# List-ordered attention on one core: how the half blocks of the transposed weights are copied, and the durations of the ordering loop

## The chip, the core and the metric

The kernel runs on one NeuronCore of a Trainium2 chip. The metric is the device time of one execution in microseconds (us), the median of a few runs. The engines are named as the profile names them: PE is the matrix engine, PEld its weight loads, DVE the vector engine, ACT the scalar engine, POOL the general engine, SP the queue that issues nearly all DMAs.

## What is computed

Three layers one after the other: causal attention with a window of 128 and a linear bias, a soft mixture of experts, and a feed-forward layer with a squared relu. All data are fp32.

```python
scores = scale * np.matmul(q, k.transpose(0, 1, 3, 2))            # (4, 8, 576, 64)
mask = (rel >= 0) & (rel < window)                                # window = 128
scores = np.where(mask, scores + bias[None], -1000000000.0)
attn = np.exp(scores - np.max(scores, axis=-1, keepdims=True))
attn = attn / (np.sum(attn, axis=-1, keepdims=True) + 1e-09)
x = np.matmul(attn, v)                                            # then (2304, 512)
x = moe(x, phi, w1, w2)                                           # 8 experts of 4 slots
out = np.maximum(x @ w_in, 0.0) ** 2 @ w_out                      # d_ff = 2048
```

## The kernel before, in words

**The attention** works on 16 units `u` (4 batches by 4 pairs of heads). A unit has 9 chunks `c` of 64 queries for both heads, so a chunk fills 128 rows. 144 chunks are taken two at a time, in 72 steps `t`; a step can hold the last chunk of one unit and the first of the next. One step goes through these functions:

- `emit_S` (L174, PE): scores of the step's two chunks, up to 192 keys each, in a bank "S" (3 of them).
- `emit_max` (L181, DVE): adds the bias table, writes the negated scores into one of six `p` buffers, and takes the row minimum in the same operation (a second small instruction reads the accumulator out).
- `emit_exp` (L192, ACT): the exponential with its row sum.
- `emit_sums` (L198, POOL) and `emit_recip` (L203, DVE): sum and reciprocal, for two steps at once except at both ends.
- `emit_fold` (L208, POOL): of the 192 keys of a chunk the oldest 64 and the newest 64 are never allowed for the same query at the same place, so the oldest are subtracted from the newest. One block then holds the newest as positive and the oldest as negative numbers, and 128 columns are left to be transposed in place of 192.
- `emit_norm` (L222, POOL): multiplies by the reciprocal.
- `emit_T` (L230, PE): transposes each chunk's 128 columns into one bank "T" (3 of them), as `A[:, i, :]`; keys are now rows.
- `emit_evac` (L251): `(t, 0)` on ACT (L254) is a Relu over all 128 rows of both chunks into the slots of `ptb`: the whole block and the newest half. `(t, 1)` on DVE then brings the oldest half, which is negative, into its slot of another block: `max(-x, 0)` on 64 rows (L258). In an even chunk these are rows 0 to 63 and in an odd one rows 64 to 127. A unit's first chunk has no older keys and its only half is copied (L260).
- `emit_PV` (L262, PE): once all of a unit's blocks are there, 24 matmuls of weights by values, each over whole slots. The half of a slot that no copy fills was set to zero at the start (L406 to L408).

Chunks 2 to 8 of a unit have an oldest half, 112 in all; 48 steps hold two of them, 16 hold one. Behind `emit_PV` come copies of its result, transposes and the logits of the experts (L281 to L379).

**The order** of all this is not the program's text. Each call is an entry `op(f, arg, eng, ns, after, due, banks, lag, at)` (L412): engine, duration in ns, what it needs, a due time, the PSUM bank that it takes, and the lag from its end until another engine may use the result. `arrange()` (L485) is a list scheduler that runs when the program is built: it repeatedly takes the entry that could start first (then the earliest due), sets its engine's clock forward by `ns` and makes the result ready `lag` later. The sequence it returns is the program's order; every engine then executes its share strictly in that order (L558). DMA issues hang on calls (L538 to L555): the last `emit_S` of a unit issues the queries and keys of a later unit and two or three half weights of 512 KB, `emit_xTb` the values of a later unit.

```python
op(emit_evac, (t, 1), "DVE", 208 * len(half), each(emit_T, t) + each(emit_evac, (t, 0)) + free(half), t0 + 4300)
...
ready[x] = max(ready[x], seen[k])
```

**After the attention** come a short softmax over experts (L588 to L665), the matmuls with w1 (L739, "H") and w2 (L878, "O"), whose 1 MB weights come through a ring of 19 tiles and are loaded again as tiles get free, and the last layer (L916 to L1120), where w_in and w_out are unpacked on the way. When the last `emit_S`, the last `emit_T` and the whole attention are done, their buffers are freed and five more weights are loaded (L97).

Of the kernel before, what the change touches and what calls it, by code (L numbers as in the profile page):

```python
# [28 lines left out]
def attn_moe_relu2_kernel(ctx: ExitStack, tc: tile.TileContext, z, k, v, phi, w1, w2, w_in, w_out, bias, cst, out):  # L29
# [200 lines left out]
    def emit_T(t):  # L230
        full, rest, P = [], [], pbuf[t % NP]
        for u, c, n, e in info[2 * t:2 * t + 2]:
            if c == 0:
                rest.append((e, 0, jblk(u, 0), False))
            elif c % 2:
                full.append((jblk(u, c // 2) + 1, e + n - 128, (64, jblk(u, c // 2 - 1) + 3, True) if c > 1 else None))
            else:
                full.append((jblk(u, c // 2 - 1) + 2, e, (0, jblk(u, c // 2), True)))
        full.sort(key=lambda x: x[0])
        A = bank("T", "tp")[:, 0:256].rearrange("p (a b) -> p a b", a=2)  # L240
        for i, o in enumerate([x[1] for x in full] + [x[0] for x in rest]):
            pe.transpose(A[:, i, :], P[:, o:o + 128], ident)  # L242
        sl = [x[0] for x in full]
        st = sl[1] - sl[0] if len(sl) == 2 else 1
        half = [(i, *x[2]) for i, x in enumerate(full) if x[2]] + [(len(full) + i, *x[1:]) for i, x in enumerate(rest)]
        tp_t[t] = (ptb[:, sl[0]:sl[-1] + 1:st], A[:, 0:len(sl)]), [(ptb[r:r + 64, slot], A[r:r + 64, i], neg) for i, r, slot, neg in half]

    def jblk(u, j):
        return 4 * ((4 * u + j) % NBL) if j < 4 else 4 * NBL + u % 2
# [177 lines left out]
    for t in range(NS):  # L427
        ch, t0 = info[2 * t:2 * t + 2], STEP * t
        two = [(t, 0), (t, 1)]
        steps = (t,) if t in alone else (t - 1, t) if t % 2 else (t, t + 1)  # L430
        op(emit_S, t, "PE", sum(4 * n / 2.4 + 12 for u, c, n, e in ch), (), t0 - 1500, (("S", each(emit_max, *two)),), 170, max(x for y, x in landed.items() if y <= t))
        for i, (u, c, n, e) in enumerate(ch):
            op(emit_max, (t, i), "DVE", n / 0.96 + 72, each(emit_S, t) + each(emit_T, *range(t - NP, t - NP + 1)[:t >= NP]), t0 + 100 * i, (), 140)
            op(emit_exp, (t, i), "ACT", n / 1.4 + 303, each(emit_max, (t, i)), t0 + 400 + 100 * i)
        if t == steps[0]:
            op(emit_sums, (t, len(steps)), "POOL", 200, each(emit_exp, *[(x, i) for x in steps for i in range(2)]), STEP * steps[-1] + 1500)
            op(emit_recip, (t, len(steps)), "DVE", 110, each(emit_sums, (t, len(steps))), STEP * steps[-1] + 1600)
        whole = sum(x[2] == 192 for x in ch)
        if whole:
            op(emit_fold, t, "POOL", 182 + 138 * whole, each(emit_exp, *two), t0 + 1500)  # L440
        for i, (u, c, n, e) in enumerate(ch):
            eng = "DVE" if t >= NS - 2 and i == 1 else "POOL"
            op(emit_norm, (t, i), eng, 345 if n > 64 else 290, each(emit_recip, (steps[0], len(steps))) + each(emit_fold, t)[:whole], t0 + 1900 + 100 * i, (), 70)
        full = [(u, (c - 1) // 2) for u, c, n, e in ch if c]
        half = [(u, c // 2 if c % 2 == 0 else c // 2 - 1) for u, c, n, e in ch if c != 1]
        free = lambda l: each(emit_PV, *[owner[x] for x in l if owner[x] is not None])
        op(emit_T, t, "PE", 222, each(emit_norm, *two), t0 + 3500, (("T", each(emit_evac, *two[:1 + bool(half)])),), 170)
        op(emit_evac, (t, 0), "ACT", 80 + 100 * len(full), each(emit_T, t) + free(full), t0 + 4000)
        if half:
            op(emit_evac, (t, 1), "DVE", 208 * len(half), each(emit_T, t) + each(emit_evac, (t, 0)) + free(half), t0 + 4300)  # L450
    for u in range(NU):
        b, kk = divmod(u, NPAIR)
        t0, odd, late = STEP * fin[u], b % 2, u == NU - 1
        parts = [(t, i) for t in range(NCH * u // 2, fin[u] + 1) for i in range(2) if (emit_evac, (t, i)) in ops]
        old = (each(emit_X, u - 4) + each(emit_logr, (u - 4) // NPAIR)) if 4 <= u < NU - 4 + 2 else []
        op(emit_PV, u, "PE", 1840, each(emit_evac, *parts), t0 + 5500, (("xa", each(emit_xT, u)), ("T" if late else "B", each(emit_xTb, u))), 190, 9500)
        op(emit_xT, u, "ACT", 490, each(emit_PV, u) + old, t0 + 7400)
        op(emit_xTb, u, "DVE" if late else "ACT", 125, each(emit_PV, u) + old, t0 + 7450)
        if late:
            break  # L460
        x_all = each(emit_xT, u) + each(emit_xTb, u)
        if u < NU - 2:
            tag = "T" if kk == NPAIR - 1 else "B"
            op(emit_X, u, "PE", 436, x_all, t0 + 9000, ((tag, each(emit_xn, u)),), 170)
            op(emit_xn, u, "DVE", 608, each(emit_X, u) + each(emit_d3, b - 1)[:b], t0 + 9500)
            if odd:
                op(emit_Y, u, "PE", 109, each(emit_X, u), t0 + 9010, (("T", each(emit_xr, u)),), 170)
                op(emit_xr, u, "ACT", 175, each(emit_Y, u) + each(emit_d3, b - 1)[:b], t0 + 9500)
        if kk == NPAIR - 1 or u == NU - 2:
            us = range(NPAIR * b, u + 1)  # L470
            x_all = each(emit_xT, *us) + each(emit_xTb, *us)
            last_b = u == NU - 2
            op(emit_logits, b, "PE", 260 * len(us) + 100, x_all, t0 + 9500, () if last_b else (("B", each(emit_d0, b)),), 190)
            op(emit_logr, b, "PE", 110 * len(us), each(emit_logits, b), t0 + 9600, (), 190)
            if last_b:
                continue
            op(emit_d0, b, "ACT", 400, each(emit_logr, b), t0 + 10500)
            op(emit_d1, b, "DVE", 600, each(emit_d0, b), t0 + 11000)
            op(emit_de, b, "ACT", 760, each(emit_d1, b), t0 + 11500)
            op(emit_d2, b, "PE", 120 + 110 * odd, each(emit_de, b), t0 + 13000, (("T", each(emit_dn, b)),), 170)  # L480
            op(emit_dn, b, "DVE", 320, each(emit_d2, b), t0 + 13500)
            op(emit_d3, b, "PE", 1260 + 500 * odd, each(emit_dn, b) + each(emit_xn, *us) + each(emit_xr, *us) * odd, t0 + 14000, (("T", each(emit_d4, b)),), 190)
            op(emit_d4, b, "DVE", 650 + 200 * (b > 0), each(emit_d3, b), t0 + 15000)

    def arrange():  # L485
        wait = {k: len(o["after"]) for k, o in ops.items()}
        for k, o in ops.items():
            for x in o["after"]:
                users.setdefault(x, []).append(k)
        ready, seen, order = {k: o["at"] for k, o in ops.items()}, {}, []  # L490
        clock = dict.fromkeys(("PE", "DVE", "ACT", "POOL"), 0)
        held = {tag: [] for tag in NBUF}
        can = {e: [k for k in ops if ops[k]["eng"] == e and not wait[k]] for e in clock}

        def room(k):
            when = 0
            for tag, readers in ops[k]["banks"]:
                if len(held[tag]) >= NBUF[tag]:
                    for x in held[tag][len(held[tag]) - NBUF[tag]]:
                        if x not in seen:  # L500
                            return None
                        when = max(when, seen[x])
            return when

        while len(order) < len(ops):
            best = None
            for e in clock:
                for k in can[e]:
                    r = room(k)
                    if r is not None:  # L510
                        x = (max(clock[e], ready[k], r), ops[k]["due"], len(order), k)
                        if best is None or x[:2] < best[:2]:
                            best = x
            start, _, _, k = best
            o = ops[k]
            can[o["eng"]].remove(k)
            clock[o["eng"]] = start + o["ns"]
            seen[k] = start + o["ns"] + o["lag"]
            for tag, readers in o["banks"]:
                held[tag].append(readers)  # L520
            for x in users.get(k, ()):
                wait[x] -= 1
                ready[x] = max(ready[x], seen[k])
                if not wait[x]:
                    can[ops[x]["eng"]].append(x)
            order.append(k)
        return order
# [644 lines left out]
```

## Time and profile before

| | us |
|---|---|
| median of 3 runs | 401.55 (401.39 to 402.41) |
| the profiled execution's own time | 401.11 |
| its span, first to last instruction | 399.3 |
| first scores to the first matmul of H | 3.7 to 137.4 |
| H and O | 137.4 to 168.0 |
| last layer | from 172 to the end |

The profile tells for each engine when it was busy. "Idle before" is the time that an engine stood before an instruction, with what ended it. The chain is found from the last instruction back: at each step to what released it, or to the instruction before it on its engine. Where a timeline shows consecutive instructions of one engine, the distance from one start to the next is what the first one costs its engine, since an instruction's own duration overlaps with the next.

### The profile page before, as it was taken

To read this page: it belongs to the slowest core of one execution; us is meant where nothing else is said; L and a number is where in the kernel's file an instruction comes from. 1 tells how busy PE (TensorE), PEld (TensorE's weight loads), DVE (VectorE), ACT (ScalarE), POOL (GpSimd) and SP (SyncE) were. 2 spreads that over 40 slices of the span, in tenths; PEclk is the share of its full clock that TensorE was granted. 3 is DMA by queue.
4 is the path that set the end of the run, shared out by engine and by line. 5 is a ranking of instruction groups with operands and counts; after the bars stand their busy time and mean duration, and the time that the engine had idled before them with its cause. 6 is when DMAs were issued, how large, how long until landed. Compare 5 with 4: busy or idle time off the path is not lost.

```text
span 399.3 us, 7923 instructions
## 1 busy us (share of the span) xinstructions
PE 387.0 (97%) x2602; PEld 300.8 (75%) x2602; DVE 283.6 (71%) x862; ACT 244.2 (61%) x730; POOL 118.0 (30%) x291
## 2 busy tenths in 40 slices
PE   8899999999998999999999999999999999999996
PEld 7687778787875534687787888788877888888884
DVE  5687787778784685477877889786867874567445
ACT  4978879778883411178867765767666634443440
POOL 4858758657674041203111111111010000000000
PEclk9999999999998999999999999999999999999999
DMA  7989969889999999999502200000000040003004
GB/s 227 384 290 340 342 244 377 303 279 379 318 365 319 389 419 423 421 417 420 193 0 77 102 34 0 2 0 2 0 0 2 0 158 2 0 27 133 0 2 158
DMA packets 23225, 75.36 MB, mean 189 GB/s; under 512 B 2832, under 2 KB 4624, under 8 KB 21520
## 3 DMA queue, kind: packets, MB, share of 16 engines
q1 hardware_dynamic: 22608, 74.30, 49.8%
q10 hardware_dynamic: 576, 0.56, 0.4%
q8 instruction: 21, 0.34, 0.3%
q14 instruction: 20, 0.16, 0.1%
HBM read 70.13 MB, written 4.72 MB: 187 GB/s over the span
## 4 chain that ended last, share of the span: by engine, by line
PE 81%; DVE 7%; ACT 5%; issue 2%; POOL 2%; DMA 2%; DVEq 0%; SPq 0%; ACTq 0%; POOLq 0%
PE acc L975 49%; PE s L178 6%; PE xa L270 4%; PE h L931 4%; PE H L739 4%; PE O L878 4%; PE tp L242 3%; ACT p L196 3%; DVE ptb L258 2%; DVE p L187 2%; DMA kt<-in_k_dram 2%; POOL p L228 1%; PE MX L827 1%; DVE psum L993 1%; ACT ptb L254 1%
## 5 line engine op out<-in xcount | busy, mean ns | idle before, releaser
L975 PE MATMUL acc<-whl,arena_gh 128*128 128x512 f32 x864 | 216.5, 394 | 0.0
L975 PEld LDWEIGHTS acc<-whl,arena_gh 128*128 128x128 f32 x864 | 160.1, 188 | 35.3 <-issue 2.9
L960 DVE TENSOR_TENSOR arena_gh<-hT,arena_gh 128x384 fp32r<-128x384 f32 (+1 forms) x97 | 53.7, 553 | 29.7 <-ACT arena_gh L956 24.2
L196 ACT ACTIVATE p<-p,st 128x192 f32<-128x192 f32 (+1 forms) x144 | 61.5, 429 | 17.0 <-DVE st L187 15.4
L943 ACT ACTIVATE acc<-h 128x384 f32<-128x384 f32 x47 | 23.1, 493 | 64.9 <-PE h L931 64.9
L787 POOL TENSOR_SCALAR yw<-f 128x512 f32<-128x512 f32 x32 | 27.3, 857 | 99.0 <-DVE arena_cin L804 53.5
L178 PE MATMUL s<-kt,zq 128*128 128x192 f32 (+2 forms) x270 | 51.0, 323 | 2.3 <-DVE st L187 1.8
L228 POOL TENSOR_SCALAR p<-p,st 128x128 f32<-128x128 f32 (+1 forms) x142 | 49.8, 370 | 11.6 <-DVE st L206 10.5
L187 DVE CUSTOM_DVE_ANT_0 p<-s,tbl 128x192 f32<-128x192 f32 (+1 forms) x144 | 41.1, 325 | 7.3 <-PE s L178 4.4
L178 PEld LDWEIGHTS s<-kt,zq 128*128 128x128 f32 x270 | 41.6, 195 | 4.2 <-DVE st L187 3.0
L258 DVE TENSOR_SCALAR ptb<-tp 64x128 f32<-64x128 f32 x112 | 32.0, 286 | 8.8 <-ACT ptb L254 6.6
L242 PE MATMUL tp<-cs,p 128*128 128x128 f32 x144 | 28.7, 288 | 3.9 <-POOL p L228 3.3
L931 PE MATMUL h<-cst_sb,Mst 128*128 128x384 f32 x95 | 32.2, 339 | 0.1
L254 ACT ACTIVATE ptb<-tp 128x256 f32<-128x256 f32 (+1 forms) x72 | 24.3, 351 | 7.7 <-PE tp L242 7.2
L220 POOL TENSOR_TENSOR p<-p 128x128 f32<-128x128 f32 (+1 forms) x64 | 27.0, 423 | 5.4 <-ACT p L196 2.6
L270 PE MATMUL xa<-ptb,vt 128*64 128x256 f32 (+1 forms) x256 | 28.6, 366 | 0.0
L196 ACT ACTIVATION_READ_ACCUMULATOR p<-p,st 128x1 f32 x144 | 27.4, 190 | 0.0
L952 DVE TENSOR_TENSOR hT<-acc 128x384 f32<-128x384 f32 x17 | 9.5, 557 | 23.6 <-ACT acc L943 23.6
L242 PEld LDWEIGHTS tp<-cs,p 128*128 128x128 f32 x144 | 17.5, 141 | 10.6 <-POOL p L228 8.1
L956 ACT ACTIVATE arena_gh<-hT 128x384 fp32r<-128x384 f32 x48 | 24.8, 516 | 0.7
L270 PEld LDWEIGHTS xa<-ptb,vt 128*64 128x64 f32 x256 | 17.3, 140 | 10.1 <-issue 2.9
L956 ACT ACTIVATE arena_gh<-acc 128x384 fp32r<-128x384 f32 x47 | 24.2, 515 | 0.6
(205 smaller groups left out, 459.4 us busy)
## 6 DMA issues: line engine op xcount, KB each, us to landing
w_w<-in_w_dram SPq DMA_DIRECT2D x38, 512.0 KB, 7.4
w_w<-in_w_dram SPq DMA_DIRECT2D x12, 1024.0 KB, 8.3
f<-in_w_in_dram SPq DMA_DIRECT2D x16, 512.0 KB, 9.9
f<-in_w_out_dram SPq DMA_DIRECT2D x16, 512.0 KB, 9.9
zq<-in_z_dram SPq DMA_DIRECT2D x13, 576.0 KB, 5.4
vt<-in_v_dram SPq DMA_DIRECT2D x16, 320.0 KB, 6.2
kt<-in_k_dram SPq DMA_DIRECT2D x13, 288.0 KB, 5.8
out_dram<-psum SPq DMA_DIRECT2D x11, 256.0 KB, 2.0
```

What stands on the lines that cost most here:

```text
L178: pe.matmul(out=sb_t[t][:, 256 * i:256 * i + n], lhsT=zbuf(u)[:, c].rearrange("p a b -> p (a b)"), rhs=kt_t[u][:, 64 * c + 64 - n:64 * c + ...
L187: dve.tensor_tensor_reduce(out=p, in0=sb_t[t][:, 256 * i:256 * i + n], in1=tbl[:, 192 * pr + 192 - n:192 * pr + 192], scale=-0.125, scalar ...
L196: act.activation(out=p, in_=p, func=AF.Exp, bias=st[:, k + i:k + i + 1], scale=-1.0, accum_out=st[:, 4 + k + i:5 + k + i])
L228: eng.tensor_scalar(out=p, in0=p, scalar1=st[:, k + i:k + i + 1], scalar2=0.0, op0=ALU.mult, op1=ALU.add)
L242: pe.transpose(A[:, i, :], P[:, o:o + 128], ident)
L254: act.activation(out=dst, in_=src, func=AF.Relu)
L258: dve.tensor_scalar(out=dst, in0=src, scalar1=-1.0, scalar2=0.0, op0=ALU.mult, op1=ALU.max)
L270: pe.matmul(out=out, lhsT=v_t[u][:, j, po:po + 64], rhs=pt[:, a:b, po:po + 64], start=(j == 0 or (j == 3 and a == 2)), stop=(j == 4 or (j ...
L931: pe.matmul(out=hb[-1][:, 0:HB], lhsT=Mst[:, 128 * f:128 * f + 128], rhs=cst_sb[:, c0:c0 + HB], start=True, stop=True)
L956: act.activation(out=lo_t[i][1][hf][:, 0, cl], in_=rbuf[hf][:, cl], func=AF.Square)
L960: eng.tensor_tensor(out=gh[hf][:, 1, cl], in0=g[hf][:, cl], in1=gh[hf][:, 0, cl].bitcast(F32), op=ALU.subtract)
L975: pe.matmul(out=acc_t[s], lhsT=gh[:, x, c0:c0 + 128], rhs=w[:, f % 2, y, :], start=(units[i] in firsts and a == 0), stop=(units[i] in last ...
```

## The change

`emit_T` prepares the copies of the half blocks in another way: where a step has oldest halves, there is one `max(-x, 0)` for it, over all 128 rows and, where there are two halves, over both chunks' 128 columns, into two slots given by one access pattern (whose step can be negative). The rows beside a half hold positive numbers or zeros, of which the operation makes zeros. The copy of a first chunk stays as it was and now stands ahead of it. In the ordering loop nearly all durations and lags get other values; the copy of halves is now put at 342 ns for two, 208 for one. And a result that is used on the engine that made it is ready at once, without the lag.

```diff
@@ -243,7 +243,15 @@
         sl = [x[0] for x in full]
         st = sl[1] - sl[0] if len(sl) == 2 else 1
         half = [(i, *x[2]) for i, x in enumerate(full) if x[2]] + [(len(full) + i, *x[1:]) for i, x in enumerate(rest)]
-        tp_t[t] = (ptb[:, sl[0]:sl[-1] + 1:st], A[:, 0:len(sl)]), [(ptb[r:r + 64, slot], A[r:r + 64, i], neg) for i, r, slot, neg in half]
+        copies = [(ptb[0:64, slot], A[0:64, i], False) for i, r, slot, neg in half if not neg]
+        neg = [(i, slot) for i, r, slot, neg in half if neg]
+        if neg:
+            to = ptb[:, neg[0][1]]
+            if len(neg) == 2:
+                a = [list(x) for x in to.ap]
+                to = bass.AP(tensor=to.tensor, offset=to.offset, ap=[a[0], [128 * (neg[1][1] - neg[0][1]), 2], [1, 128]])
+            copies.append((to, A[:, neg[0][0]:neg[-1][0] + 1] if len(neg) == 2 else A[:, neg[0][0]], True))
+        tp_t[t] = (ptb[:, sl[0]:sl[-1] + 1:st], A[:, 0:len(sl)]), copies
 
     def jblk(u, j):
         return 4 * ((4 * u + j) % NBL) if j < 4 else 4 * NBL + u % 2
@@ -428,34 +436,34 @@
         ch, t0 = info[2 * t:2 * t + 2], STEP * t
         two = [(t, 0), (t, 1)]
         steps = (t,) if t in alone else (t - 1, t) if t % 2 else (t, t + 1)
-        op(emit_S, t, "PE", sum(4 * n / 2.4 + 12 for u, c, n, e in ch), (), t0 - 1500, (("S", each(emit_max, *two)),), 170, max(x for y, x in landed.items() if y <= t))
+        op(emit_S, t, "PE", sum(4 * n / 2.4 + 12 for u, c, n, e in ch), (), t0 - 1500, (("S", each(emit_max, *two)),), 200, max(x for y, x in landed.items() if y <= t))
         for i, (u, c, n, e) in enumerate(ch):
-            op(emit_max, (t, i), "DVE", n / 0.96 + 72, each(emit_S, t) + each(emit_T, *range(t - NP, t - NP + 1)[:t >= NP]), t0 + 100 * i, (), 140)
-            op(emit_exp, (t, i), "ACT", n / 1.4 + 303, each(emit_max, (t, i)), t0 + 400 + 100 * i)
+            op(emit_max, (t, i), "DVE", n / 0.96 + 72, each(emit_S, t) + each(emit_T, *range(t - NP, t - NP + 1)[:t >= NP]), t0 + 100 * i, (), 108)
+            op(emit_exp, (t, i), "ACT", n / 1.4 + 303, each(emit_max, (t, i)), t0 + 400 + 100 * i, (), 170)
         if t == steps[0]:
-            op(emit_sums, (t, len(steps)), "POOL", 200, each(emit_exp, *[(x, i) for x in steps for i in range(2)]), STEP * steps[-1] + 1500)
-            op(emit_recip, (t, len(steps)), "DVE", 110, each(emit_sums, (t, len(steps))), STEP * steps[-1] + 1600)
+            op(emit_sums, (t, len(steps)), "POOL", 274, each(emit_exp, *[(x, i) for x in steps for i in range(2)]), STEP * steps[-1] + 1500, (), 0)
+            op(emit_recip, (t, len(steps)), "DVE", 90, each(emit_sums, (t, len(steps))), STEP * steps[-1] + 1600, (), 120)
         whole = sum(x[2] == 192 for x in ch)
         if whole:
-            op(emit_fold, t, "POOL", 182 + 138 * whole, each(emit_exp, *two), t0 + 1500)
+            op(emit_fold, t, "POOL", 164 + 138 * whole, each(emit_exp, *two), t0 + 1500)
         for i, (u, c, n, e) in enumerate(ch):
             eng = "DVE" if t >= NS - 2 and i == 1 else "POOL"
-            op(emit_norm, (t, i), eng, 345 if n > 64 else 290, each(emit_recip, (steps[0], len(steps))) + each(emit_fold, t)[:whole], t0 + 1900 + 100 * i, (), 70)
+            op(emit_norm, (t, i), eng, 350 if n > 64 else 290, each(emit_recip, (steps[0], len(steps))) + each(emit_fold, t)[:whole], t0 + 1900 + 100 * i, (), 80)
         full = [(u, (c - 1) // 2) for u, c, n, e in ch if c]
         half = [(u, c // 2 if c % 2 == 0 else c // 2 - 1) for u, c, n, e in ch if c != 1]
         free = lambda l: each(emit_PV, *[owner[x] for x in l if owner[x] is not None])
-        op(emit_T, t, "PE", 222, each(emit_norm, *two), t0 + 3500, (("T", each(emit_evac, *two[:1 + bool(half)])),), 170)
-        op(emit_evac, (t, 0), "ACT", 80 + 100 * len(full), each(emit_T, t) + free(full), t0 + 4000)
+        op(emit_T, t, "PE", 222, each(emit_norm, *two), t0 + 3500, (("T", each(emit_evac, *two[:1 + bool(half)])),), 200)
+        op(emit_evac, (t, 0), "ACT", 52 + 106 * len(full), each(emit_T, t) + free(full), t0 + 4000, (), 135)
         if half:
-            op(emit_evac, (t, 1), "DVE", 208 * len(half), each(emit_T, t) + each(emit_evac, (t, 0)) + free(half), t0 + 4300)
+            op(emit_evac, (t, 1), "DVE", (0, 208, 342)[sum(x[1] > 1 for x in ch)] + 208 * sum(x[1] == 0 for x in ch), each(emit_T, t) + each(emit_evac, (t, 0)) + free(half), t0 + 4300, (), 120)
     for u in range(NU):
         b, kk = divmod(u, NPAIR)
         t0, odd, late = STEP * fin[u], b % 2, u == NU - 1
         parts = [(t, i) for t in range(NCH * u // 2, fin[u] + 1) for i in range(2) if (emit_evac, (t, i)) in ops]
         old = (each(emit_X, u - 4) + each(emit_logr, (u - 4) // NPAIR)) if 4 <= u < NU - 4 + 2 else []
         op(emit_PV, u, "PE", 1840, each(emit_evac, *parts), t0 + 5500, (("xa", each(emit_xT, u)), ("T" if late else "B", each(emit_xTb, u))), 190, 9500)
-        op(emit_xT, u, "ACT", 490, each(emit_PV, u) + old, t0 + 7400)
-        op(emit_xTb, u, "DVE" if late else "ACT", 125, each(emit_PV, u) + old, t0 + 7450)
+        op(emit_xT, u, "ACT", 477, each(emit_PV, u) + old, t0 + 7400, (), 165)
+        op(emit_xTb, u, "DVE" if late else "ACT", 104, each(emit_PV, u) + old, t0 + 7450, (), 165)
         if late:
             break
         x_all = each(emit_xT, u) + each(emit_xTb, u)
@@ -520,7 +528,7 @@
                 held[tag].append(readers)
             for x in users.get(k, ()):
                 wait[x] -= 1
-                ready[x] = max(ready[x], seen[k])
+                ready[x] = max(ready[x], seen[k] if ops[x]["eng"] != o["eng"] else clock[o["eng"]])
                 if not wait[x]:
                     can[ops[x]["eng"]].append(x)
             order.append(k)
```

## Rows read from the trace of the kernel before

**Rows 1.** Windows: stretch, length, busy us of each engine, clock, DMA share.

```profile
core 0: us, PE busy (x) PEld busy (x) DVE busy (x) ACT busy (x) POOL busy (x), PEclk, DMA share, GB/s
17.00:131.00 114.00, 109.87 (x1034) 86.93 (x1034) 83.64 (x437) 88.55 (x373) 75.99 (x222) 0.99 0.92 325
...
137.40:172.70 35.30, 35.26 (x440) 18.01 (x441) 23.62 (x66) 7.86 (x19) 8.85 (x10) 1.00 1.01 420
```

**Rows 2.** The chain of waits, 17 to 131 us: shares by line.

```profile
by line: PE s L178 16.3%; PE xa L270 15.3%; PE tp L242 9.5%; ACT p L196 9.1%; DVE ptb L258 7.8%; issue 6.7%; DVE p L187 5.7%; DMA kt<-in_k_dram 3.7%; PE L L300 2.9%; ACT ptb L254 2.6%; PE X L313 2.4%; POOL p L228 2.2%; DVE xn_all L321 2.1%;
```

**Rows 3.** Waits, 17 to 131 us: us in total, times, longest.

```profile
POOL st L201 <- ACT p L196: 16.5, 15, 3.1
ACT p L196 <- DVE st L187: 12.2, 18, 1.3
DVE ptb L258 <- ACT ptb L254: 5.7, 11, 1.3
```

**Rows 4.** The page's group of the half copies: count, busy us, mean ns.

```profile
L258 DVE TENSOR_SCALAR ptb<-tp 64x128 f32<-64x128 f32 x112 | 32.0, 286 | 8.8 <-ACT ptb L254 6.6
```

**Rows 5.** Timeline of DVE around pairs of half copies: start, length, what.

```profile
57.75 0.69 DVE L321 COPY xn_all<-X 128x512 f32<-128x512 f32 x1
58.35 0.35 DVE L187 CUSTOM_DVE_ANT_0 p<-s,tbl 128x192 f32<-128x192 f32 x1
...
58.67 0.61 DVE L258 TENSOR_SCALAR ptb<-tp 64x128 f32<-64x128 f32 x2
59.31 0.36 DVE L187 CUSTOM_DVE_ANT_0 p<-s,tbl 128x192 f32<-128x192 f32 x1
...
82.14 0.61 DVE L258 TENSOR_SCALAR ptb<-tp 64x128 f32<-64x128 f32 x2
82.67 0.34 DVE L187 CUSTOM_DVE_ANT_0 p<-s,tbl 128x192 f32<-128x192 f32 x1
...
82.95 0.68 DVE L321 COPY xn_all<-X 128x512 f32<-128x512 f32 x1
83.66 0.61 DVE L258 TENSOR_SCALAR ptb<-tp 64x128 f32<-64x128 f32 x2
```

**Rows 6.** Timeline of DVE: single copies from PSUM, on 64 and on 128 rows.

```profile
60.15 0.28 DVE L258 TENSOR_SCALAR ptb<-tp 64x128 f32<-64x128 f32 x1
60.35 0.27 DVE L260 COPY ptb<-tp 64x128 f32<-64x128 f32 x1
...
78.31 0.29 DVE L359 COPY dn<-X 128x128 f32<-128x128 f32 x1 [0.98 <-PE X L355]
78.52 0.18 DVE L361 COPY dn<-X 128x32 f32<-128x32 f32 x1
```

**Rows 7.** Timeline of POOL: the sums and what follows them.

```profile
62.74 0.19 POOL L201 TENSOR_SCALAR st<-st 128x4 f32<-128x4 f32 x1
63.02 0.46 POOL L220 TENSOR_TENSOR p<-p 128x128 f32<-128x128 f32 x1
```

**Rows 8.** The chain piece by piece: start, length, what.

```profile
28.34 4.17 DMA kt<-in_k_dram
...
60.92 1.67 PE xa L270 x16
...
127.18 2.50 PE xa L270 x16
```

**Rows 9.** Windows, as rows 1, around the attention's end.

```profile
126.00:132.00 6.00, 6.00 (x55) 4.13 (x54) 1.98 (x7) 1.95 (x6) 0.29 (x1) 0.76 0.85 283
```

**Rows 10.** The last w2 load, issued at 154.4 us, and its time to landing.

```profile
L70 SPq DMA_DIRECT2D w_w<-in_w_dram x1: 328/328/328, 154.4 to 154.4; - x1
...
DMA to landing us min/median/max: 11.6/11.6/11.6
```

**Rows 11.** The chain: the last 13 of O's 16 weights (16 matmuls each).

```profile
156.69 11.36 PE O L878 x208
```

**Rows 12.** Waits of the DMA queue, 90 to 135 us.

```profile
SPq L97 <- PE tp L242: 6.0, 1, 6.0
```

## The prediction, made before the change was run

> **What bounds the kernel now.** I read the windows first, to see which engine fills which stretch, then the chain of waits, the waits, and last the timeline of DVE. The change touches the attention alone. Between 17 and 131 us PE is marked busy for 109.9 of 114 us, DVE 83.6, ACT 88.6, POOL 76.0 [rows 1]. Taken alone, this says that PE bounds the stage. The chain says something else: the scores, PV and the transposes make 41% of it, and with the logits' and X's matmuls PE has about 46%; the rest changes hands between ACT, DVE, POOL and short issue times [rows 2]. So the stage is not filled by one engine; it is four queues executed strictly in order, which meet again and again. DVE is on the chain with the half copies (7.8%), the maxima (5.7%) and the copies of X (2.1%) [rows 2], and ACT stood 12.2 us, in 18 waits, for DVE's maxima [rows 3].
>
> [...]
>
> I go by the chain; that PE's row is right as it stands is part of a rival below.
>
> **What a pair of half copies costs now.** The page's group has 112 of them at a mean of 286 ns, but that overlaps with what follows [rows 4]. The distance between starts is the price to the queue. A single copy of rows 0 to 63 takes 0.20 us from its start to the next one's (60.15 to 60.35) [rows 6]. A pair takes more than twice that: from 58.67 to the maximum at 59.31 are 0.64 us, and the pair at 82.14 took 0.53 until 82.67 [rows 5]. In the second kind the missing tenth lies in front: the copy of X at 57.75 let a maximum start after 0.60 us, the one at 82.95 let a pair start only after 0.71 [rows 5]. The reading that fits both: a copy on rows 64 to 127 starts late behind an operation that begins at row 0, and what follows it starts late too; which half comes first only decides where this is paid. Every pair has one half on rows 64 to 127, so I take 0.62 us for each of the 48.
>
> **What the new operation costs.** No row shows 128x256 elements from PSUM on DVE. The nearest are 128 elements at 0.20 and 512 at 0.60 (57.75 to 58.35) [rows 5, 6]: 0.40 us for 384 elements, so 0.20 + 128 x 0.00104 = 0.335 us. That it has 128 rows instead of 64 costs nothing: a 128-row copy from PSUM took 0.21 to the next start (78.31 to 78.52) [rows 6]. It begins at row 0 like everything around it, so nothing is held. Bounds: 0.335 at best; 0.53 at worst, the cheaper pair of today, if two slots in one pattern cost as two operations. I take 0.34, since the rows on both sides of the size lie on a line.
>
> [...]
>
> **The sum.** Per pair 0.62 - 0.34 = 0.28 us, 48 times: 13.4 us less in DVE's queue. The 16 single ones go from 64 to 128 rows at no cost (row above), the 16 plain copies stay; in the steps that hold both, only their order is swapped. No DMA is added or moved by this part.
>
> Most of the 13.4 us falls into time that DVE waits anyhow: it is idle for 30 of the 114 us [rows 1]. What counts is the part on the chain. The half copies hold 7.8% of 114 us there, 8.9 us [rows 2]; of each pair 0.28 of 0.62, or 45%, goes: 4.0 us. Behind them, maxima come earlier and ACT's waits for them get shorter. Not all of it stays: as soon as a pair leaves the chain, another line ends next. What is late then is ACT's exponentials (9.1% of the chain) and, behind them, POOL's sums, which already stood 16.5 us for ACT [rows 2, 3]. I keep three quarters, 3.0 us. Bounds: 0, if everything is late by the same amount elsewhere, and 4.0 plus a third of the 12.2 us that ACT stood for DVE [rows 3], so 8.
>
> **A joined wait.** The pair now waits for both slots to be read by older PVs and for ACT's Relu, where the first half could go as soon as its own slot was free. Already now the first half waits for ACT (5.7 us in 11 waits) [rows 3], and the loop asked for all slots in any case. If a slot is late, the maxima of the next step are queued behind it on DVE and ACT behind those. Price: at most the first half's 0.3 us, in some of the 16 units; I put it at 0 because the saved 0.28 covers it.
>
> **The new order.** All other edits change the sequence only. The old loop put a pair at 2 x 208 = 416 ns, while rows 5 show 0.62; the new one has 342, close to my 0.34. The POOL sums go from 200 to 274; the rows have 0.28 [rows 7]. Lags get longer, a same-engine result is ready at once. So the list comes nearer to what the chip does. What it moves can't be read from a profile: PE's, DVE's, ACT's and POOL's calls, and with `emit_S` and `emit_xTb` the loads of queries, keys, half weights and values on SP. Bounds by the rows: the idle issue time (6.7%) and POOL's norms (2.2%) on the chain, 10 us together [rows 2], of which a third might go, -3 us; and one more key load on the chain like that at 28.34, +4.2 us [rows 8]. Between these I take 0.
>
> PE's clock is a small unknown too. [...]
>
> **Does it reach the end?** Behind the attention DMA is full: 420 GB/s and a share of 1.01 until 172.7 us [rows 1]. The last w2 load lands at 154.4 + 11.6 = 166.0 us [rows 10]; its matmuls start when 12 of the last 13 weights are done, at 156.7 + 12/13 x 11.4 = 167.2 [rows 11]. The slack is 1.2 us. A gain of 3 us passes only if the stream of loads begins earlier as well. It should: the loads behind the attention waited 6.0 us for the last transposes [rows 12], which come earlier, and the share before was 0.92 at 325 GB/s [rows 1]. The last layer is not touched and follows as it is.
>
> So the profiled execution's 401.1 becomes 398.1. The runs' median is 0.4 above that execution, and I forecast **398.5 us**.
>
> **The rivals.** About 0.3%, 1.2 us, is what a measurement of this kernel can tell from no change.
>
> *The gain is swallowed, 400.7 us.* Either PE is the bound that its row shows, and the pairs leave a chain that has another of equal length beside it; or the weight stream does not move with the attention, and O then waits for its last weight, so that 1.2 us at most pass. For it: 109.9 of 114, and the slack of 1.2 us. Against: less than half the chain is PE, and the issue of the loads hangs on the attention's end. Of the 3.0 us between 0.5 and 1.2 are left then; 0.85 makes 400.7.
>
> *More than the pairs, 395.5 us.* The list plans with prices that hold, and the waits around POOL's sums and norms shrink as well: the 3.0 us and the 3 us bound of the order together. For it: the plan was off by 0.2 us in 48 steps. Against: nothing shows that the rest of the order is bad.
>
> *Slower, 405 us.* The reordered list lets `emit_S` run further ahead, since it sees transposes and copies ready later by the longer lags. Queries and keys have two buffers, and their loads are issued when an older unit's scores are done. If the scores reach a unit before its keys have landed, PE's queue stands with everything behind it. One such load lies on the chain at 28.34 for 4.17 us [rows 8]. Two such stalls of 4.2 take 8.4; with the gain of 3 and some 2 that run beside other work anyhow, 3.4 us are lost, 405. The case decides when a load is later than its scores by more than the 3 us gained, summed over the units. Against: key loads make 3.7% of the chain's 114 us [rows 2], which is this one piece and no other.
>
> *The change does not do what it says, 400.2 us.* If the joined copy takes 0.53, a pair saves 0.09, or 15% of 8.9, 1.3 us on the chain, and the loop's 342 would be wrong again. Nothing in the rows points to it; its chance is in the swallowed case's.
>
> **How the numbers follow.** Forecast 0.53, swallowed 0.18, more 0.15, slower 0.14. The first and third are faster, 0.68; the second is within 0.3%; the last is slower. The time is that of the likeliest. Its own range, by the share kept of the 4.0 us and the clock, is 396.5 to 400.3. For eight in ten the range runs from 394.9, just beyond the case of more, to 402.6, where the slower case begins, leaving out about 0.06 below and 0.14 above.
>
> **What would show it.** Right: 64 half copies instead of 112, a pair at 0.34 to its next start, DVE some 13 us less busy in the attention or that much more idle, L258's share of the chain down to 4% or less, H's first matmul at about 134.4 instead of 137.4 us, and its distance to the end unchanged. Wrong: a pair at 0.5 us; H no earlier (another queue took it); H earlier but O waiting for a weight; or key loads and ACT's waits grown, which would be the order's doing.

## The result, and the profile after

The changed kernel takes **395.93 us** (median of 4 runs, 395.53 to 398.23) against 401.47 in the same comparison: a ratio of 0.988 (95% interval 0.983 to 0.992). A second comparison, with 6 runs against 23 of before, gave 395.85 us and **0.987** (0.985 to 0.989): 5.2 us less. The forecast was 398.5.

The windows after, as [rows 1], with the attention's end moved to 126 us, and the same stretch as in [rows 9], in which the attention is over by now:

```profile
17.00:126.00 109.00, 105.79 (x1041) 86.02 (x1039) 75.22 (x393) 90.74 (x376) 75.96 (x222) 1.00 0.94 338
...
126.00:132.00 6.00, 5.27 (x46) 3.44 (x49) 3.77 (x16) 2.63 (x8) 0.00 (x0) 1.00 0.98 392
```

DVE has 75 us of work where it had 84; PE has 86.0 us of weight loads where it had 86.9, in 5 us less. The chain of waits, 17 to 126 us, as [rows 2]:

```profile
by line: PE s L178 29.5%; PE xa L278 21.4%; PE tp L242 14.3%; DMA kt<-in_k_dram 12.5%; PE X L321 5.5%; PE L L308 3.1%; PE xb L278 3.0%; PE R L374 2.7%; PE L L314 2.0%; PE X L603 1.1%; issue 1.0%; PE X L363 0.8%; PE R L377 0.8%; SPq L149 0.6
```

Of DVE, ACT and POOL, whose half copies, maxima, exponentials and norms had a quarter of the chain, no line is left in the part listed. It is now PE, and the loads of keys with 12.5% instead of 3.7%. The waits, 17 to 126 us, as [rows 3], show the same from the other side:

```profile
POOL st L201 <- ACT p L196: 8.8, 13, 1.5
DVE ptb L266 <- ACT ptb L262: 7.8, 11, 1.4
...
ACT p L196 <- DVE st L187: 3.1, 5, 1.3
PEld s L178 <- DMA zq<-in_z_dram: 2.9, 2, 1.9
...
PE s L178 <- DMA kt<-in_k_dram: 2.4, 2, 1.6
```

ACT stands 3.1 us for DVE's maxima and no longer 12.2, POOL 8.8 for ACT and no longer 16.5; what is new are 2.4 us, in two waits, in which PE stands for keys. The 2.9 us in which its weight loads stand for queries, which are issued just ahead of the keys, are the same two places.

The half copies, as [rows 4] (page) and [rows 5] (timeline of DVE):

```profile
L266 DVE TENSOR_SCALAR ptb<-tp 128x256 f32<-128x256 f32 (+1 forms) x64 | 24.4, 385 | 8.2 <-ACT ptb L262 8.0
```

```profile
61.97 0.69 DVE L329 COPY xn_all<-X 128x512 f32<-128x512 f32 x1
62.58 0.75 DVE L266 TENSOR_SCALAR ptb<-tp 128x256 f32<-128x256 f32 x2
63.24 0.35 DVE L187 CUSTOM_DVE_ANT_0 p<-s,tbl 128x192 f32<-128x192 f32 x1
```

64 instead of 112. Two joined copies take 0.66 us from 62.58 to the next maximum, 0.33 each; one pair of single copies took 0.62. The copy of X in front lets go after 0.61 us and not 0.71.

Behind the attention (timeline of PE in before and after, then the chain after):

```profile
137.40 7.07 PE L739 MATMUL H<-w_w,siT 128*32 128x512 f32 x64
144.26 1.07 PE L739 MATMUL H<-yw,siT 128*32 128x512 f32 x8
```

```profile
131.72 7.07 PE L747 MATMUL H<-w_w,siT 128*32 128x512 f32 x64
138.94 1.06 PE L747 MATMUL H<-yw,siT 128*32 128x512 f32 x8
```

```profile
126.53 12.37 DMA yw<-in_w_dram
...
138.94 1.92 PE H L747 x16
```

H begins at 131.72 us and not at 137.40: 5.7 us earlier. Its ninth weight, `yw`, is the last that is loaded behind the attention; its matmuls start 7.22 us after the first of H, against 6.86 in before (144.26), as they now have to wait until it lands. That gives 0.4 us back; from there to the end the two kernels take the same time, 255 us.

### The profile page after: what moved, and what is told of

Same layout as the page of the kernel before. It is cut to its first block, busy times and chain, and to the rows that moved or that the text cites. A ratio compares the mean times of both kernels' runs of the same rounds, so it can differ in the third digit from the quotient of the medians.

```text
span 394.0 us, 7876 instructions
## 1 busy us (share of the span) xinstructions
PE 383.5 (97%) x2602; PEld 299.9 (76%) x2602; DVE 273.8 (69%) x814; ACT 245.7 (62%) x730; POOL 118.0 (30%) x291
## 4 chain that ended last, share of the span: by engine, by line
PE 88%; DMA 7%; DVE 2%; POOL 1%; ACT 1%; issue 1%; SPq 0%; DVEq 0%; POOLq 0%; ACTq 0%
PE acc L983 49%; PE s L178 10%; PE xa L278 6%; PE h L939 4%; DMA kt<-in_k_dram 4%; PE tp L242 4%; PE O L886 4%; DMA yw<-in_w_dram 3%; PE H L747 2%; PE X L321 2%; PE MX L835 1%; DVE psum L1001 1%; PE L L308 1%; PE xb L278 1%; PE R L374 1%
## 5 line engine op out<-in xcount | busy, mean ns | idle before, releaser
L228 POOL TENSOR_SCALAR p<-p,st 128x128 f32<-128x128 f32 (+1 forms) x142 | 49.9, 371 | 16.2 <-DVE st L206 10.7
L187 DVE CUSTOM_DVE_ANT_0 p<-s,tbl 128x192 f32<-128x192 f32 (+1 forms) x144 | 42.1, 324 | 10.2 <-PE s L178 6.1
L266 DVE TENSOR_SCALAR ptb<-tp 128x256 f32<-128x256 f32 (+1 forms) x64 | 24.4, 385 | 8.2 <-ACT ptb L262 8.0
L242 PE MATMUL tp<-cs,p 128*128 128x128 f32 x144 | 26.7, 282 | 2.2 <-POOL p L228 2.0
L278 PE MATMUL xa<-ptb,vt 128*64 128x256 f32 (+1 forms) x256 | 27.8, 359 | 0.0
L810 DVE SCALAR_TENSOR_TENSOR yw<-f,yw 128x512 int32<-128x512 int32 x32 | 22.4, 706 | 0.8
```

Source lines behind the costliest of these rows:

```text
L187: dve.tensor_tensor_reduce(out=p, in0=sb_t[t][:, 256 * i:256 * i + n], in1=tbl[:, 192 * pr + 192 - n:192 * pr + 192], scale=-0.125, scalar ...
L228: eng.tensor_scalar(out=p, in0=p, scalar1=st[:, k + i:k + i + 1], scalar2=0.0, op0=ALU.mult, op1=ALU.add)
L278: pe.matmul(out=out, lhsT=v_t[u][:, j, po:po + 64], rhs=pt[:, a:b, po:po + 64], start=(j == 0 or (j == 3 and a == 2)), stop=(j == 4 or (j ...
```

## The experiments

Each was compared with the kernel before on the same chip; ratios are to that kernel, with 95% intervals.

### Joined copies alone, and the new loop alone

The first keeps the old loop and so the order of every engine; only `emit_T` is the changed one.

```diff
 # kernel before
-        tp_t[t] = (...), [(ptb[r:r + 64, slot], A[r:r + 64, i], neg) for i, r, slot, neg in half]
+        copies = ...
+        tp_t[t] = (...), copies
```

> The joined copies alone, with the old loop and so the old order on every engine. If the pairs' price in DVE's queue makes most of the gain: 397.5 to 398.5 us (3 us less than before, the forecast's sum). If the new order makes it: above 400.3 us. DVE's busy time in the attention falls by about 8 us in both cases.

Measured: 397.62 us, ratio **0.993** (0.990 to 0.996), by which it is 2.8 us less. The other half of the change is the reverse of it: the changed kernel with `emit_T` of before.

> The new loop alone, so the order of after, but the halves copied singly as before. If the order makes the gain by itself: below 398.5 us. If the order is worth something only with copies that are as cheap as it believes: 400 us or more, since each pair then runs 0.28 us behind the plan.

Measured: 399.95 us, **0.998** (0.996 to 1.000), 0.9 us less, next to the second case. So the copies make about half of the gain. The two alone add up to 0.991, and together they give 0.987: by these ratios the order is worth some 2.3 us with cheap copies, 0.9 without. The intervals just reach the case that the two only add up, and part of both numbers belongs to PE's clock (see The low clock).

The chains, 17 to 122 us, of before, with the joined copies alone, and with the new loop alone:

```profile
by line: PE s L178 17.7%; PE xa L270 14.3%; ACT p L196 9.4%; PE tp L242 9.3%; DVE ptb L258 8.5%; issue 7.0%; DVE p L187 6.2%; DMA kt<-in_k_dram 4.0%; PE X L313 2.6%; ACT ptb L254 2.4%; DVE xn_all L321 2.3%; POOL p L228 2.1%; PE xb L270 2.0%
```

```profile
by line: PE s L178 27.4%; PE xa L278 19.0%; DMA kt<-in_k_dram 17.7%; PE tp L242 11.9%; PE X L321 5.0%; PE L L308 2.9%; PE R L374 2.8%; PE xb L278 2.6%; PE L L314 1.6%; ACT p L196 1.4%; issue 1.3%; PE X L363 0.8%; DVE ptb L266 0.8%; PE R L37
```

```profile
by line: ACT p L196 13.5%; DVE ptb L258 11.6%; PE s L178 11.2%; DVE p L187 7.9%; PE xa L270 7.9%; issue 7.5%; DMA kt<-in_k_dram 6.6%; PE tp L242 5.5%; DVE xn_all L321 3.2%; POOL p L228 3.1%; PE L L300 2.9%; ACT ptb L254 2.9%; PE X L313 2.1%
```

With the copies alone, the half copies shrink from 8.5% to 0.8% and ACT's exponentials from 9.4% to 1.4%; PE and the key loads, with 17.7% for 4.0%, take their place. With the loop alone, DVE and ACT hold the chain, more than in before.

### Is it the joining, or the first row?

The kernel before, with its two copies a pair, but each over all 128 rows. The order is that of before on every engine.

```diff
 # kernel before
-        ... [(ptb[r:r + 64, slot], A[r:r + 64, i], neg) for i, r, slot, neg in half]
+        ... [(ptb[:, slot], A[:, i], neg) if neg else (ptb[0:64, slot], A[0:64, i], neg) for i, r, slot, neg in half]
```

> The old loop and two copies a pair, but each over all 128 rows. If the extra 0.2 us of a pair comes from starting at row 64 between operations that start at row 0, the distance from start to start falls to 0.20 us for every copy, a pair to 0.41, and the time goes most of the way of the joined copies alone (a third of their saving is then left to joining: 0.07 of 0.28 us). If it came from two writes into one tile or from the wait for ACT, the pair stays at 0.53 to 0.64 us and the time at 401.5 us.

Measured: 398.24 us, **0.993** (0.990 to 0.995), as with the joined copies. The timeline of DVE at the same place in before and in this run:

```profile
55.92 1.23 DVE L258 TENSOR_SCALAR ptb<-tp 64x128 f32<-64x128 f32 x4
57.19 0.36 DVE L187 CUSTOM_DVE_ANT_0 p<-s,tbl 128x192 f32<-128x192 f32 x1
```

```profile
55.06 0.97 DVE L258 TENSOR_SCALAR ptb<-tp 128x128 f32<-128x128 f32 x4
55.95 0.35 DVE L187 CUSTOM_DVE_ANT_0 p<-s,tbl 128x192 f32<-128x192 f32 x1
```

Four copies, two pairs, take 0.89 us to the next start: 0.22 each, 0.45 a pair, where the two pairs of before take 1.27. The work per copy has doubled in rows, and it is faster. The order is that of before; what differs is the rows, and all copies now start at row 0. A single copy of rows 0 to 63 took 0.20 in before as well [rows 6]. So what a pair paid for was a start at row 64 between operations that start at row 0: 0.64 us fall to 0.45, about 0.2 us for a pair. What in the engine takes this time is not shown.

The same was tried on the changed kernel, with the loop told 416 ns for two copies.

```diff
 # changed kernel: emit_T with the line above, and
-            op(emit_evac, (t, 1), "DVE", (0, 208, 342)[...] + ...
+            op(emit_evac, (t, 1), "DVE", (0, 208, 416)[...] + ...
```

> The new loop with two copies a pair, each over all 128 rows, and the loop told 416 ns for two. If starting at row 0 is what counts and joining adds nothing, as with the old loop (0.9929 against 0.993): 0.988, as the changed kernel. If joining counts once the order is right: 0.990 to 0.992.

Measured: 396.99 us, 0.989 (0.987 to 0.992). That lies between the two cases, and the changed kernel's 0.987 lies within the interval. What joining adds is 0.2% by these two and can't be told from nothing; their intervals would also allow about 0.5%.

### What the loop knows

Joined copies with the old loop, but the new price of the copies; then the new loop with single copies, told 620 ns for a pair; then the changed kernel without the rule for results of the same engine.

```diff
 # kernel before, with the joined copies
-            op(emit_evac, (t, 1), "DVE", 208 * len(half), ...
+            op(emit_evac, (t, 1), "DVE", (0, 208, 342)[...] + ...
 # changed kernel, with the single copies
-            op(emit_evac, (t, 1), "DVE", (0, 208, 342)[...] + ...
+            op(emit_evac, (t, 1), "DVE", (0, 208, 620)[...] + ...
 # changed kernel
-                ready[x] = max(ready[x], seen[k] if ops[x]["eng"] != o["eng"] else clock[o["eng"]])
+                ready[x] = max(ready[x], seen[k])
```

> Joined copies, and of the loop only their price (342 and 208 in place of 208 for each half). If the extra of both together comes from the loop knowing the price of the copies: as the whole change, 0.988. If it comes from the other durations and lags: as the joined copies alone, 0.993, or anything near, since the order is another one.

> The new loop with single copies, as in the run of the loop alone, but told that a pair costs 620 ns. If the loop alone gained little (0.998) because it believed in 342: now 0.993 to 0.995. If DVE's time itself is what stands in the way: 0.998 again, or slower.

> The changed kernel, but a same-engine result again counts as ready only after its lag. If this rule carries part of the order's gain: 0.99 or above. If it only swaps neighbours (a transpose before or after a small one): 0.988, within 0.2% of the changed kernel.

Measured: 397.7 us, 0.992 (0.990 to 0.995); 401.02 us, 1.000 (0.998 to 1.003); 396.7 us, 0.989 (0.986 to 0.992). By its ratio the price of the copies alone does not bring the order's gain, which then needs the other durations and lags; how much of it they carry stays rough, since eight of that run's twelve executions had the lower mean clock (see The low clock), and the other four, at 396.6 us, are only 0.7 us behind the changed kernel. Telling the loop the true price of dear copies doesn't help either. In that run ACT stands for DVE nearly as in before (waits, then the chain, 17 to 122 us):

```profile
ACT p L196 <- DVE st L187: 10.0, 14, 1.2
```

```profile
by line: PE s L178 21.4%; PE xa L270 14.3%; DMA kt<-in_k_dram 10.7%; PE tp L242 9.5%; ACT p L196 6.1%; DVE ptb L258 5.7%; issue 4.9%; PE X L313 3.7%; DVE p L187 3.4%; PE L L300 2.9%; POOL p L228 2.7%; DVE xn_all L321 2.5%; PE xb L270 2.0%; 
```

The number is the one expected if DVE's time itself is in the way. That this is the reason is not shown: the half copies have less of the chain than in before (5.7% for 8.5%), and the key loads more (10.7% for 4.0%). The rule for the same engine can't be told from nothing.

### What the order changed: one place

PE's timeline around the third unit's PV, in before, with the joined copies alone, and after, and the first matmul of H with the joined copies alone:

```profile
31.89 0.49 PE L178 MATMUL s<-kt,zq 128*128 128x192 f32 x2
32.65 0.41 PE L178 MATMUL s<-kt,zq 128*128 128x64 f32 x2 [0.26 <-DMA kt<-in_k_dram]
32.98 1.73 PE L270 MATMUL xa<-ptb,vt 128*64 128x256 f32 x16
```

```profile
30.94 0.49 PE L178 MATMUL s<-kt,zq 128*128 128x192 f32 x2
32.31 0.41 PE L178 MATMUL s<-kt,zq 128*128 128x64 f32 x2 [0.88 <-DMA kt<-in_k_dram]
32.64 1.73 PE L278 MATMUL xa<-ptb,vt 128*64 128x256 f32 x16
```

```profile
28.02 1.26 PE L178 MATMUL s<-kt,zq 128*128 128x64 f32 x8
29.21 1.74 PE L278 MATMUL xa<-ptb,vt 128*64 128x256 f32 x16
```

```profile
133.49 7.07 PE L747 MATMUL H<-w_w,siT 128*32 128x512 f32 x64
```

The old list put all scores of the fifth unit in front of that PV, and the first of the sixth, whose keys were still on the way (the 4.17 us piece of [rows 8]); with cheaper copies PE only stood there longer, 0.88 us instead of 0.26. The new list has 8 of the fifth unit's 18 matmuls ahead of PV and the others behind it, and PV starts 3.4 us earlier than with the joined copies alone. When H begins, the changed kernel is 1.8 us ahead (131.72 against 133.49). That these 1.8 us come from this place is not shown: with the new loop alone PV starts early too, at 30.36 us, and that kernel gains little.

### Are the key loads the next bound?

In the changed kernel the longest stall of PE stood here (timelines of PE and of the DMA queue):

```profile
91.86 0.49 PE L178 MATMUL s<-kt,zq 128*128 128x192 f32 x2
93.99 1.66 PE L178 MATMUL s<-kt,zq 128*128 128x64 f32 x10 [1.65 <-DMA kt<-in_k_dram]
```

```profile
81.06 0.42 SPq L88 DMA_DIRECT2D w_w<-in_w_dram  x1
81.53 0.43 SPq L82 DMA_DIRECT2D w_w<-in_w_dram  x1
82.01 0.46 SPq L88 DMA_DIRECT2D w_w<-in_w_dram  x1
82.89 0.33 SPq L160 DMA_DIRECT2D vt<-in_v_dram  x1
86.29 0.33 SPq L149 DMA_DIRECT2D zq<-in_z_dram  x1
86.67 1.20 SPq L156 DMA_DIRECT2D kt<-in_k_dram  x1
```

Three half weights and a value load are issued 3.4 to 5.2 us ahead of the queries, in the same queue, and the keys follow the queries. The two key loads on the chain, issued at 56.77 and 86.67 us, each came 6.1 us behind the key load before, with three half weights in between, and took 6.4 and 7.2 us from issue to landing, where the median is 5.5; two longer intervals, of 7.7 and 8.5 us, had only two. So they were spread otherwise, on three kernels, 38 in all as before:

```diff
-                    for _ in range(0 if u == 0 else 3 if u % 2 == 0 or u == 15 else 2):
+                    for _ in range(0 if u == 0 else 3 if u % 4 < 2 or u == 15 else 2):
```

> The changed kernel, but of the 38 half weights in the attention three instead of two are issued behind units 1, 5, 9, 13 and two instead of three behind units 2, 6, 10, 14, so that fewer stand in the DMA queue in front of the key loads that follow 6 us later. If late query and key loads are what bounds the attention now (PE stood 2.4 us for them): 394 us, one to two us less than the changed kernel, and PE's waits for kt nearly gone. If these waits are only taken over by another queue: 395.9 us as before.

> The joined copies with the old loop and the half weights spread as in the run beside it. If the joined copies alone stopped at 0.993 because PE then waits for keys (3.2 us): 0.988 to 0.990. If it is the old order itself: 0.993 again.

> Before, with the half weights spread in the same way. PE waited 0.3 us for keys there, so if the key loads only became the bound through the cheaper copies: 401 us, no change (within 0.2%). If the loads already held the attention back in before: 399 us or less.

Measured: on the changed kernel 395.09 us, **0.985** (0.983 to 0.988); on the joined copies alone 396.52 us, **0.989** (0.987 to 0.992), where it was 0.993; on before 401.16 us, **1.000** (0.998 to 1.002). The same edit is worth nothing before and 1.5 us with the joined copies, though the intervals of these two runs just overlap. With the chains above, this says that the key loads became a bound through the cheaper copies. The chain of the changed kernel with the spread weights, 17 to 122 us:

```profile
by line: PE s L178 34.5%; PE xa L278 25.1%; PE tp L242 16.3%; PE X L321 6.1%; PE xb L278 3.3%; PE L L308 2.9%; PE R L374 2.8%; PE L L314 1.9%; issue 1.3%; PE X L363 0.8%; PE R L377 0.8%; DVE ptb L266 0.7%; PE Y L325 0.6%; DVE xn_all L329 0.
```

No key load is left in it, and the attention is PE's. But the time falls by 0.8 us only, less than expected. H begins 1.6 us earlier than in the changed kernel, at 130.09, and then waits for its ninth weight (timeline of PE, then the chain):

```profile
130.09 7.07 PE L747 MATMUL H<-w_w,siT 128*32 128x512 f32 x64
138.07 1.06 PE L747 MATMUL H<-yw,siT 128*32 128x512 f32 x8 [0.90 <-DMA yw<-in_w_dram]
```

```profile
124.91 13.12 DMA yw<-in_w_dram
138.03 0.04 issue
138.07 1.92 PE H L747 x16
```

The matmuls with `yw` start 7.98 us after the first of H, 1.1 us later than in before. This is the fastest version measured; its lead on the changed kernel, measured in another set, is smaller than the intervals.

### The low clock

> Before, with five matmuls of the identity into a bank that is free by then, behind the transposes of step 69, where PE stood 1.3 us in before (1.2 us of work into that gap). [...]

```diff
 # kernel before
+        if f is emit_T and a == NS - 3:
+            keep_warm("S", 5)
```

Measured: 400.65 us, 0.999 (0.996 to 1.001). The granted clock (windows):

```profile
14.00:20.00 6.00, 5.17 (x35) 4.05 (x36) 3.22 (x19) 4.40 (x20) 4.70 (x15) 0.72 1.04 411
120.00:132.00 12.00, 11.59 (x126) 8.47 (x126) 7.30 (x31) 6.55 (x25) 5.19 (x15) 1.00 0.94 311
```

A gain of 1 to 1.5 us was expected if the low clock at the end of the attention came of the gap there; the gain is less. The granted clock is now 1.00 in 120 to 132 us, where before had 0.50 from 125.5 to 128.5 us, but in this execution it was 0.72 in 14 to 20 us instead. In before PE stands 1.29 us in that stretch too, until 15.19 us, at a clock of 1.00. The changed kernel's execution has no such stretch in the attention (1.00 from 17 to 126 us); the profiled one of before has it, and there its last PV took 0.8 us longer than the one at 60.92 [rows 8].

One profile doesn't price this, but the mean granted clock of every execution is on record. It is either 0.996 or less, or 0.998 or more. Of 75 executions of before, 45 have the lower mean (median 401.4 us) and 30 the higher (400.2). With the five matmuls 2 of 12 have the lower; the other 10 take 400.2 us, as those of before at the higher mean. So what filling the gap gains goes with the clock alone: 1.2 us between an execution at the lower mean and one at the higher.

The changed kernel halves that gap (timeline of PE, before and after):

```profile
124.44 0.44 PE L242 MATMUL tp<-cs,p 128*128 128x128 f32 x2 [1.32 <-POOL p L228]
```

```profile
120.10 0.44 PE L242 MATMUL tp<-cs,p 128*128 128x128 f32 x2 [0.65 <-POOL p L228]
```

All ten of its executions have the higher mean. Compared with the executions of before that have it too, each within its own set, the whole change is worth 4.3 us, the joined copies alone 2.6 and the new loop alone 0.2, each good to some half a us. By this split about 0.9 of the 5.2 us is the clock's, and the order itself is worth about 1.7 us with the joined copies and next to nothing without. Whether the shorter gap is what keeps the clock up is not shown: with the joined copies alone, in the order of before, 10 of 12 executions had the higher mean.

## Why the prediction was right, and where not

**The price of a pair** was right: 0.62 us before, 0.33 after for 0.34 forecast. The rows on both sides of the size held for the distance between starts; the joined copy's own recorded length is 0.42 us. The reading of why a pair cost that much, a start at row 64, was shown by the run on all rows, where a pair took 0.45 us.

**The pairs on the chain**: three quarters of 4.0, 3.0 us, were forecast; the joined copies alone gave 2.8. The size held, but in part by luck. The sum let 45% of the half copies' share go, and in the run nearly all of it went. What I named as late next was not it: ACT's exponentials fell to 1.4% of the chain, and of POOL, which still stood 15.6 us for ACT, no line is listed. PE's own work and the key loads took over.

**The new order**, "Between these I take 0", is the term that was mis-sized. By the ratios the order is worth 0.9 us alone and about 2.3 with the joined copies; at the same mean clock it is 0.2 and 1.7, inside the bounds of a gain of 3 and a loss of 4.2 us. PE's clock was also taken as 0, with 1 us to either side in the range: no run shows that 1 us. In its place the runs showed 1.2 us between executions of before at the lower and the higher mean, and some 0.9 of the whole gain. So the whole gain came out 5.2 instead of 3.0. The rows had one such place: the key load at 28.34 on the chain. I read it as the price of a worse order, when it was what a better one could take away; how much of the gain it carries is not shown. The rival that counted on it (two such stalls, slower) had the right mechanism in part: PE did come to wait for keys, but for 2.4 us in all, and the cheap copies brought this and not the new order, since with the old one it was 3.2 us.

**More than the pairs**, 395.5 us, was the case that came true, at a chance of 0.15. Its number is near partly by luck, since it had nothing for the clock. Its reason, prices that hold in the list, is shown only in part: POOL's sums stand 8.8 us for ACT and no longer 16.5, but its norms stand for the reciprocals as before (9.4 and 9.5 us); the price of the copies alone gave 0.992, and the rule for the same engine can't be told from nothing.

**Does it reach the end**: the stream of weights did begin earlier, as forecast, and 5.3 of the 5.7 us passed. What has no slack is not the last w2 weight but `yw` in H; the 1.2 us computed for the former said nothing on it.

**The signs named in advance**: 64 copies, found; 13 us less in DVE's queue shows as some 8 us less busy time, since lengths are not distances: two single copies have a recorded 0.57 us for 0.62 in the queue, a joined one 0.42 for 0.33; no half copy in the listed chain where 4% was allowed; H at 131.7 for 134.4. Of the signs of being wrong, grown waits for keys were seen, 2.4 us for 0.3, but with the old order too, so they are not the order's doing.

## What to carry to other kernels

What an instruction costs its queue is the distance to the next start, and that depends on its neighbours: here a copy of X on DVE let go after 0.60 us ahead of a maximum and after 0.71 ahead of a pair [rows 5]. On DVE, try to let operations that follow each other begin at the same row, even if rows are written for nothing: here that brought a pair from 0.64 to 0.45 us. When an engine leaves the chain, look at once for what takes its place, here loads of 288 KB in a queue behind ones of 512 KB; the edit that fixes it can be worth nothing before. And price an order's bounds by naming what stands on the chain that the order could remove, not only what it could add.

## What was not expected of the hardware

A copy of twice the rows was faster than one of half: 0.22 us on 128 rows against 0.26 to 0.32 on 64, the mean of the two in a pair, of which one starts at row 64. And the low clock does not stand at one place: 6 of the 14 profiled executions have a mean granted clock of 0.996 or less. Windows of four show where. In before it is 0.50 from 125.5 to 128.5 us, behind PE's gap of 1.32 us; with the joined copies and only their price in the loop, and with the single copies over all rows in the new loop, 0.86 in 118 to 130 us; with the gap filled, 0.72 in 14 to 20 us. A gap does not bring it each time: PE stands 1.29 us until 15.19 us in before and 1.35 until 15.16 in the changed kernel, and both have a clock of 1.00 in 14 to 20 us.
